# Pooled attention and a gated MLP on one core: the prologue as written words in another order, a packing product with its operands exchanged, a third output buffer, and shifted places in the later batches

## The chip, the cores and the metric

The kernel runs on one core of a Trainium2 chip. The metric is the device time of one execution in microseconds (us): for the kernel before, 744.43 as the median of three runs (742.96 to 745.0). The profile was taken from an execution of its own. TensorE (PE) multiplies matrices and writes to PSUM; VectorE (DVE) and ScalarE (ACT) read PSUM and SBUF; SyncE (SP) issues nearly all transfers.

## The reference

Eight batches of eight heads, 576 rows, head size 64, and 32 packing queries p per head, all float32:

```python
p_packed = sm_attn(p, k, v)          # softmax(p k^T / 8) v : 32 x 64 per head
out = sm_attn(q, p_packed, p_packed) # softmax(q p_packed^T / 8) p_packed : 576 x 64 per head
x = out.transpose(0, 2, 1, 3).reshape(4608, 512)
g = x @ w_gate                       # 512 x 1536
y = (g * sigmoid(g) * (x @ w_val)) @ w_out
```

## The kernel before

**Products without x.** The second softmax's weights a2 multiply p_packed, and that goes straight into w_gate and w_val. So the kernel forms m = p_packed times the weights for each batch (`m_mm`, L561) and then gate and value as m with a2 (`gv_chunk`, L602; `gv`, L788, for batch 0). The weights' 1536 columns are 12 chunks (`fc`); for each chunk a batch's 576 rows are done in two parts, A (256 columns of a2) and B (320). Then `silu`, the product with the value, and the product with w_out into four accumulators (`out_mm`, L633; `outs`, L836). Float32 accuracy comes from splitting each operand into a high and a low half (mh/ml, a2h/a2l, hh/hl, wo_h/wo_l) and adding three products; chunks 0 to 3 of batch 0 use the plain float32 product for gate and value (L801) and chunks 0 to 9 for w_out (L842). A plain product is issued as two instructions.

**Packing.** Batches 0 and 1 go by `s1_*`: scores with the 32 queries of each head on the partitions, their maximum, exp, transpositions on TensorE (`s1_turn`, L305, copied out by `s1_turned`), the product with v (`s1_pack`, L324), the sums, the division (`s1_scale`, L348), a transposition (`s1_flip`) and a copy (`s1_ppt`) into `ppt`. Batches 2 to 7 go by `q_*`: scores in four stretches of rows, maxima and sums kept by stretch (`q_sums`), gathered through DRAM (`q_gather`, L415), joined (`q_common`, L424), multiplied into the weights and transposed on VectorE in blocks of 32 (`q_turn`, L450), and then `q_pack` (L462): for each head pair (4) and each block of 32 rows (5), four products with the weights' block as stationary operand (128 rows by 32 columns) and 32 columns of v as moving operand. Each of the four writes its own 32 partitions of PSUM. VectorE transposes the result in blocks of 32 into `ppt`.

**Second softmax.** `s2_mm` (L487, two halves of 288 rows), `s2_block` (transposition of the scores by blocks), `s2_max`, `s2_exp`, `s2_sums`, `s2_scale`, and the transposition back. In batch 0 the latter is `back` (L768), which writes `a2f`.

**Weights.** They arrive as 64-bit floats. `f64_convert` (L181) makes float32 of a chunk in five steps, two on ScalarE (L187, L188) and three on VectorE (L189, L190, L191). In the written orders `W2` is the next step of chunk 2 of gate and value, `V0` of pair 0 of w_out.

**What sets the order.** Up to the end of batch 0 the orders of TensorE, VectorE, ScalarE and SP are those of the text. First come calls written one by one (L718 to L778), the prologue: loads, 8 warm-up matmuls of the identity with itself (`warm_up`, L702, each two instructions), the packing of batch 0, five steps of W0, the second softmax's first half, 18 more warm-ups. Then the words of `PROGRAM` (L40) are run in order (L896); its numbers say chunk, half or part. `g5` is the sixth gate-and-value part, `silu5` and `h5` its evaluation, `out5` its product with w_out, `M:1.0` a product m, `Mh:`/`Ml:` its high and low halves, `two_*` the second softmax of batch 0, `s1_*` and `s2_*` batch 1's, `warm25` 25 warm-ups.

From batch 1 on TensorE's order stays that of the text, and the other engines' instructions are ordered by a planner, save those held behind their predecessor in the text (`pin`, L154). The tables `FIRST` (for batch 2) and `LATER` (batches 3 to 7) say at which place of the batch before each part of a batch's attention is put: chunk and place within it, 1 and 2 in A's gate and value, a and ha behind A's silu and high half, 3 and 4 in A's out, 5 to 8, b and hb the same for B (`words2`, L650; `plan_of`, L685; called from `batch`, L912).

**Buffers.** PSUM has four accumulators, two `gv` and two `aux` buffers; while `wide` is true (the prologue) small products take accumulators and gv buffers in turn (`ps`, L158). Copies of finished accumulators go to `ot` (`emit_out`, L643), two buffers, and from there to DRAM.

Of the kernel before, what the change touches and what calls it, by code (L numbers as in the profile page):

```python
# [10 lines left out]
F32 = mybir.dt.float32  # L11
# [4 lines left out]
ALU = mybir.AluOpType  # L16
# [5 lines left out]
NP = 32  # L22
DM, DF = 512, 1536
P = 128
# [16 lines left out]
    W2 g0 W1 two_max1 two_high0 W2 warm25 W1 two_exp1 W2 W2 silu0 V0 h0 W2 V0 W1 load_w3 load_v1 M:1.0 two_sums1  # L41
    Mh:1.0 M:0.1 V0 Mh:0.1 two_scale1 g1 V0 silu1 two_back1 s1_scores0 h1 g2 two_high1 s1_max0 W3 V0 load_w4
    load_w5 silu2 W3 W3 out0 h2 s1_keep0 W3 g3 two_low1 silu3 W3 s1_scores1 load_wout1 load_w6 h3 g4 s1_max1 W4
    two_low0 out1 s1_top s1_keep1 W4 silu4 W4 h4 M:1.1 W5 W4 g5 Mh:1.1 W5 W5 W4 load_w7 out2 silu5 V1 h5 W5 out3
    V1 V1 g6 W5 load_wout2 W6 V1 silu6 M:2.2 W6 h6 g7 V1 load_w8 Mh:2.2 silu7 W6 W7 Ml:2.2 out5 W7 W7 h7 g8 V2 W7
    silu8 out4 V2 V2 W7 out6 W8 V2 W8 out7 W8 V2 g9 h8 s1_exp W6 out8 W6 load_w9 load_wout3 load_w10 W8 M:3.2
    silu9 h9 out9 Mh:3.2 W8 load_wout4 Ml:3.2 g10 silu10 s1_turn0 h10 g11 s1_turned0 W9 silu11 s1_turn1 W9 W9
    out10 h11 s1_turned1 W9 V3 out11 V3 V3 W9 load_w11 g12 W10 V3 M:4.2 silu12 W10 h12 g13 V3 load_q1 Mh:4.2 W10
    silu13 out12 V4 h13 Ml:4.2 V4 g14 V4 silu14 V4 W11 s1_turn2 out13 s1_turned2 h14 W11 W11 W10 s1_pack W10
    load_wout5 g15 s1_sums silu15 V4 load_k2 load_v2 out14 h15 W11 g16 silu16 W11 s1_flip out15 s1_ppt h16 V5  # L50
# [9 lines left out]
    0.b q0r  # L60
    0.hb q0s
    1.2 q0e
    1.ha q1 q1r
    2.a q1e
    2.7 q0z
    2.8 q1z
    3.2 common
    3.a common_e factors
    4.5 load_k
    4.b turn0  # L70
    4.hb turn1
    5.ha pack
    6.b load_v
    6.7 tiles
    7.ha mm0 block0
    7.3 max0
    8.a exp0 sums0
    8.7 turn_0
    9.ha mm1 block1
    9.3 high0 low0  # L80
    9.hb max1 exp1
    9.7 load_q
    9.8 sums1
    10.hb turn_1
    11.3 high1
    11.hb low1
# [18 lines left out]
    7.3 max0  # L105
    7.7 load_v
# [3 lines left out]
    9.a high0  # L110
    9.ha mm1 block1
    9.b low0
    9.hb max1 exp1
    9.7 load_q
    10.1 sums1
    10.hb turn_1
    10.8 high1
    11.4 low1
# [4 lines left out]
def tile_pack_attention_swiglu(ctx: ExitStack, tc: tile.TileContext, qT, kT, v, vq, pT, wgv, wout, out):  # L123
# [30 lines left out]
    def pin(ins):  # L154

        return tc.keep_in_program_order(ins) if steady[0] else ins
# [305 lines left out]
    def q_pack(b, bank=ps):  # L462

        p_p = bank()
        a1, v_t = sq[b][4], vs[b]
        for hp in range(NHP):
            for k in range(NKQ):
                for g in range(P // NP):
                    par, ds = g // 2, slice(g % 2 * NP, g % 2 * NP + NP)
                    nc.tensor.matmul(  # L470
                        p_p[NP * g : NP * g + NP, NP * hp : NP * hp + NP],
                        a1[:, par, hp, k, :], v_t[:, par, hp, k, ds],
                        start=(k == 0), stop=(k == NKQ - 1),
                    )
# [224 lines left out]
    with tc.manual_schedule(engines={mybir.EngineType.PE}):  # L699
# [15 lines left out]
        with tc.manual_schedule(  # L715
            engines={mybir.EngineType.DVE, mybir.EngineType.Activation, mybir.EngineType.SP}
        ):
            load_k(0)  # L718
            load_w(0)
            load_v(0)  # L720
            load_q(0)
            load_w(1)
            warm_up(8)
            s1_tile(0)
            for hf in range(2):
                s1_scores(0, hf)
                s1_max(0, hf)
            load_w(2)
            warm_up(6)
            s1_top(0)  # L730
            s1_exp(0, True)
            for x in range(NPAR + 1):
                s1_turn(0, x)
                s1_turned(0, x, nc.vector)
            s1_pack(0)
            s1_sums(0, True)
# [8 lines left out]
            for _ in range(4):  # L745
                step("W", 0)
            s1_scale(0)
            step("W", 0)
            s1_flip(0)
            s1_ppt(0)  # L750
            s2_tiles(0)
            c0, c1 = (slice(c, c + 1) for c in range(2))
            s2_mm(0, 0)
            s2_block(0, 0)
            m_mm(0, 0, c0, True)
            m_high(0, 0, c0)
            s2_max(0, c0)
            s2_exp(0, c0)
            s2_mm(0, 1)
            s2_block(0, 1)  # L760
            load_k(1)
            load_wout(0)
            warm_up(18)
            step("W", 1)
            step("W", 1)
            a2f = pool.tile([P, NPAR, S], F32, tag="a1", bufs=1, name="a2f")

            def back(c):  # L768
                for par in range(NPAR):
                    nc.vector.transpose(a2f[:, par, c * HS : (c + 1) * HS], st2[0][0][:, c, par])  # L770

            s2_sums(0, c0)
            s2_scale(0, c0)
            back(0)
            wide[0] = False

            t4_of(0)
            rows, accs = accs_of(0)  # L778
# [9 lines left out]
            def gv(i):  # L788
# [3 lines left out]
                if k < PLAIN:  # L792
                    terms = ((ms[0, k][0], a2f),)
# [53 lines left out]
            def a2_high(c):  # L847
                if c == 0:
                    s2_a2(0)
                nc.scalar.copy(a2[0][0][s2_at(c)], a2f[s2_at(c)])  # L850

            def a2_low(c):
                nc.vector.tensor_tensor(
                    a2[0][1][s2_at(c)], a2f[s2_at(c)], a2[0][0][s2_at(c)].bitcast(F32), op=ALU.subtract
                )
# [14 lines left out]
            def half_of(f, b):  # L870
# [7 lines left out]
                "g": gv, "silu": silu, "h": hmul, "hh": h_high, "hl": h_low, "out": outs,  # L878
                "W": lambda k: step("W", k), "V": lambda k: step("V", k),
# [149 lines left out]
```

## Time and profile before

| | |
|---|---|
| median of three runs | 744.43 us (742.96 to 745.0) |
| profiled execution, its time and its span | 742.52 us, 740.7 us |
| TensorE busy | 726.7 us, 98% |
| TensorE weight loads | 595.3 us, 80% |
| VectorE, ScalarE busy | 448.8 us (61%), 372.1 us (50%) |
| DMA traffic | 59.16 MB |
| granted TensorE clock | 1.000 |

A row of a group reads: line, engine, operation, output<-inputs, shapes, count. In a timeline the first two numbers are start and length in us; a bracket at the end holds the engine's idle time just before and what ended it. "issue" is idle time in which the engine waited for nothing that the profile shows. PEld is TensorE's loading of stationary operands, which runs beside the matmuls. In the chain of waits each row is start, length, and what was waited for.

### The profile page before, as it was taken

The page shows a single profiled execution, that of the slowest core. Times are in us where ns is not written, and L with a number is a line of the kernel's source. Part 1 is how long each engine was busy: PE and PEld are TensorE (multiplying, and loading weights), DVE is VectorE, ACT ScalarE, POOL GpSimd, SP SyncE. Part 2 cuts the span into 40 slices and gives each one's busy share as a digit, 9 for nine tenths or more (in the row PEclk, how much of TensorE's full clock was granted, in tenths as well). Part 3 has the DMA queues.
Part 4 walks back from the last instruction along what each step waited for, and adds up shares of the span by engine and source line. Part 5 has one row for each costly group of instructions (what it writes and reads, how often), then busy time and mean ns, then how long its engine had stood idle before and what let it go on. Part 6 is the DMA issues. An engine that isn't in the chain of part 4 may idle for free.

```text
span 740.7 us, 15176 instructions
## 1 busy us (share of the span) xinstructions
PE 726.7 (98%) x6288; PEld 595.3 (80%) x6288; DVE 448.8 (61%) x1008; ACT 372.1 (50%) x666; POOL 2.0 (0%) x13
## 2 busy tenths in 40 slices
PE   7999999999999999999999999999999999999997
PEld 5756667888888888888888888888888888888885
DVE  5988878675755557654665646655574545644333
ACT  3777745744635345553563536663553625533331
POOL 0000000000000000000000000000000000000000
PEclk9999999999999999999999999999999999999999
DMA  9686582310112201302112021102001000010001
GB/s 352 254 322 252 181 325 86 102 59 17 65 58 85 74 1 65 125 4 73 65 44 97 3 73 65 58 3 73 1 1 72 3 2 1 1 58 1 1 1 72
DMA packets 20005, 59.16 MB, mean 80 GB/s; under 512 B 5984, under 2 KB 7008, under 8 KB 17376
## 3 DMA queue, kind: packets, MB, share of 16 engines
q1 hardware_dynamic: 19792, 58.12, 21.7%
q8 instruction: 50, 0.82, 0.5%
q14 instruction: 19, 0.16, 0.1%
q10 hardware_dynamic: 144, 0.07, 0.0%
HBM read 48.69 MB, written 9.49 MB: 79 GB/s over the span
## 4 chain that ended last, share of the span: by engine, by line
PE 95%; DVE 2%; issue 1%; DMA 0%; ACT 0%; DVEq 0%; ACTq 0%
PE gv L616 36%; PE acc L635 33%; PE aux L257 7%; PE gv L801 6%; PE acc L842 4%; PE aux L635 4%; PE gv_aux L470 1%; PE gv_aux L257 1%; PE gv_aux L386 1%; PE acc L704 1%; DMA out<-ot 0%; DVE ot L170 0%; ACT mh L583 0%; PE aux L333 0%; DVE s L529 0%
## 5 line engine op out<-in xcount | busy, mean ns | idle before, releaser
L623 ACT ACTIVATE sg<-gv 128x256 f32<-128x256 f32 (+1 forms) x168 | 68.9, 410 | 173.8 <-PE gv L616 155.8
L627 DVE TENSOR_TENSOR hf<-gv,sg 128x256 f32<-128x256 f32 x168 | 71.0, 422 | 135.0 <-PE gv L616 116.6
L616 PE MATMUL gv<-a2h,ml 128*128 128x256 f32 (+1 forms) x672 | 143.9, 296 | 1.2 <-DVE t L826 1.2
L616 PE MATMUL gv<-a2h,mh 128*128 128x256 f32 (+1 forms) x672 | 144.1, 296 | 0.0
L616 PE MATMUL gv<-a2l,mh 128*128 128x256 f32 (+1 forms) x672 | 144.0, 296 | 0.0
L635 PE MATMUL acc<-wo_h,hl 128*128 128x512 f32 x344 | 140.7, 409 | 0.0
L635 PE MATMUL acc<-wo_l,hh 128*128 128x512 f32 x344 | 135.7, 395 | 0.0
L635 PE MATMUL acc<-wo_h,hh 128*128 128x512 f32 x344 | 134.7, 391 | 0.0
L616 PEld LDWEIGHTS gv<-a2h,ml 128*128 128x128 f32 x672 | 116.8, 189 | 16.3 <-issue 1.4
L168 ACT CAST hh<-hf 128x256 fp32r<-128x256 f32 x168 | 67.8, 404 | 106.4 <-DVE hf L627 106.3
L616 PEld LDWEIGHTS gv<-a2h,mh 128*128 128x128 f32 x672 | 108.6, 190 | 0.1
L616 PEld LDWEIGHTS gv<-a2l,mh 128*128 128x128 f32 x672 | 108.2, 189 | 0.0
L597 DVE TENSOR_TENSOR hl<-hf,hh 128x256 fp32r<-128x256 f32 x168 | 69.5, 414 | 37.6 <-ACT hh L168 37.6
L635 PEld LDWEIGHTS acc<-wo_h,hl 128*128 128x128 f32 x344 | 64.7, 188 | 27.6 <-issue 18.6
L635 PEld LDWEIGHTS acc<-wo_h,hh 128*128 128x128 f32 x344 | 64.6, 188 | 14.9
L635 PEld LDWEIGHTS acc<-wo_l,hh 128*128 128x128 f32 x344 | 64.8, 188 | 8.1 <-issue 0.5
L557 DVE TENSOR_TENSOR ml<-aux,mh 128x512 fp32r<-128x512 f32 x92 | 58.8, 680 | 2.4 <-ACT mh L583 2.4
L583 ACT CAST mh<-aux 128x512 fp32r<-128x512 f32 x92 | 49.4, 589 | 9.6 <-PE aux L257 4.3
L257 PE MATMUL aux<-w,ppt 64*32 64x512 f32 (+1 forms) x784 | 52.4, 588 | 0.5 <-ACT mh L583 0.5
L623 ACT ACT_TABLE_LOAD x30 | 38.5, 1283 | 12.3 <-PE gv L616 11.8
L842 PE MATMUL acc<-wo_f,h 128*128 128x512 f32 x80 | 37.2, 595 | 0.0
L842 PEld LDWEIGHTS acc<-wo_f,h 128*128 128x128 f32 x80 | 14.3, 189 | 13.8 <-issue 13.2
(152 smaller groups left out, 754.7 us busy)
## 6 DMA issues: line engine op xcount, KB each, us to landing
st<-in_wgv SPq DMA_DIRECT2D x12, 1024.0 KB, 6.5
k_t<-in_kT SPq DMA_DIRECT2D x16, 576.0 KB, 5.1
q_t<-in_qT SPq DMA_DIRECT2D x16, 576.0 KB, 4.8
out<-ot SPq DMA_DIRECT2D x36, 256.0 KB, 2.1
v_t<-in_vq SPq DMA_DIRECT2D x6, 1280.0 KB, 5.9
st<-in_wout SPq DMA_DIRECT2D x6, 1024.0 KB, 5.5
v_t<-in_v SPq DMA_DIRECT2D x2, 1024.0 KB, 8.7
p_t<-in_pT SPq DMA_DIRECT2D x7, 64.0 KB, 2.6
```

Of the source, the lines that this page charges most:

```text
L168: e.copy(dst, src)
L257: nc.tensor.matmul(outs[par][32 * hp : 32 * hp + 32], lhs(r, hp), rhs(r, hp), start=True, stop=True)
L386: nc.tensor.matmul(pss[par][NP * j : NP * j + NP, i * SQ : (i + 1) * SQ], p_t[r, 2 * g + i, :], k_t[r, j // 2, 2 * g + i, j % 2 * SQ : j % ...
L557: pin(nc.vector.tensor_tensor(*lows.pop(0), op=ALU.subtract))
L583: nc.scalar.copy(m[0][at], src)
L597: low = lo.tensor_tensor(hl, src, hh.bitcast(F32), op=ALU.subtract)
L616: nc.tensor.matmul(pg[:, :n], m_[:, g, f, s * P : (s + 1) * P], a_[:, g, off : off + n], start=(i == 0), stop=(i == 5),)
L623: nc.scalar.activation(sg[:, :n], pgs[0][:, :n], AF.Silu)
L627: nc.vector.tensor_tensor(hf, pgs[1][:, o : o + 256], sg[:, o : o + 256], op=ALU.mult)
L635: nc.tensor.matmul(acc[:, :], h_[:, c : c + P], w_[fc // 2][:, fc % 2], start=(fc == 0 and i == 0), stop=(fc == NFC - 1 and i == 2),)
L801: nc.tensor.matmul(held[i][s][:, :n], m_[:, g, f, s * P : (s + 1) * P], a_[:, g, off : off + n], start=(j == 0), stop=(j == len(todo) - 1),)
L842: nc.tensor.matmul(accs[2 * is_b + c], half(i)[:, c * P : c * P + P], wos[fc // 2][:, fc % 2], start=(fc == 0), stop=(fc == NFC - 1),)
```

## The change

1. The prologue's calls become words at the head of `PROGRAM` (`z_*` for batch 0's packing, `two_mm`, `two_block`, `heat` for the warm-ups, `narrow` for the end of the wide use of PSUM), and the whole order is another one. `back` makes its tile when first called.
2. `q_pack` takes v as stationary operand (128 rows by 64 columns) and the weights' block as moving operand (32 columns), so that the product comes out transposed; a copy replaces VectorE's transposition.
3. `ot` has three buffers.
4. `FIRST` and `LATER` hold other places.

```diff
 PROGRAM = """
-    W2 g0 W1 two_max1 two_high0 W2 warm25 W1 two_exp1 W2 W2 silu0 V0 h0 W2 V0 W1 load_w3 load_v1 M:1.0 two_sums1
-    Mh:1.0 M:0.1 V0 Mh:0.1 two_scale1 g1 V0 silu1 two_back1 s1_scores0 h1 g2 two_high1 s1_max0 W3 V0 load_w4
...
-    M:5.2 wout_high0 V5 g17 wout_high1 wout_low0 wout_high2 wout_low1 silu17 wout_low2 V5 out16 h17 Mh:5.2 V5 g18
-    wout_high3 Ml:5.2 silu18 out17 h18 V5 g19 wout_low3 silu19 wout_high10 s2_mm0 h19 g20 s2_block0 silu20
-    wout_high11 s2_mm1 load_q2 h20 hh20 wout_low10 s2_max0 g21 hl20 silu21 out19 h21 hh21 s2_block1 out20 s2_max1
-    s2_exp0 wout_low11 s2_exp1 hl21 s2_sums1 g22 M:6.2 s2_back1 silu22 out18 Mh:6.2 h22 hh22 s2_sums0 s2_high1
-    out21 Ml:6.2 hl22 s2_low1 g23 s2_back0 silu23 h23 hh23 s2_high0 hl23 s2_low0
+    load_k0 load_w0 load_v0 load_q0 z_scores0 z_scores1 z_max0 z_max1 z_top heat8 load_w1 load_w2 load_k1 heat6
+    z_exp z_turn0 z_turned0 z_turn1 z_turned1 z_turn2 W0 W0 z_turned2 z_sums W0 load_wout0 z_pack z_scale z_flip
+    W0 z_ppt two_mm1 two_mm0 W0 two_block0 two_max0 two_exp0 two_block1 two_sums0 M:0.0 two_scale0 heat18 narrow
+    two_max1 W1 Mh:0.0 W1 W2 two_back0 g0 W1 two_exp1 two_high0 W2 W2 silu0 V0 W1 V0 W2 load_v1 W2 warm25 W1
+    load_w3 M:1.0 M:0.1 two_sums1 h0 two_scale1 Mh:1.0 V0 Mh:0.1 two_back1 g1 s1_scores0 silu1 load_w5 V0 g2
...
+    M:5.2 out16 Mh:5.2 g18 silu18 h17 Ml:5.2 wout_low2 h18 g19 wout_low3 V5 s2_mm0 silu19 g20 wout_high10 h19
+    wout_low1 wout_high11 load_q2 silu20 s2_block0 g21 h20 wout_low10 hh20 s2_mm1 silu21 hl20 s2_max0 h21 hh21
+    s2_block1 out19 g22 s2_max1 s2_exp1 s2_exp0 wout_low11 out20 s2_sums1 hl21 silu22 out17 s2_back1 M:6.2 out18
+    Mh:6.2 s2_high1 h22 g23 s2_sums0 s2_low1 silu23 Ml:6.2 h23 hh22 s2_back0 hh23 hl23 s2_high0 hl22 s2_low0
+    out21
 """
 FIRST = """
...
+    1.6 q0z
     2.a q1e
-    2.7 q0z
-    2.8 q1z
-    3.2 common
+    2.4 q1z
+    3.a common
...
 LATER = """
...
-    1.4 q0z
     2.a q1e
-    2.4 q1z
-    3.ha common
-    3.5 common_e
-    3.hb factors
-    4.a turn0
-    4.4 load_k
-    4.5 turn1
+    2.6 q0z
+    2.b q1z
+    2.7 common
+    3.2 common_e
+    3.4 factors
+    3.7 load_k turn0
+    4.ha turn1
     5.ha pack
...
@@ def q_pack
-                for g in range(P // NP):
-                    par, ds = g // 2, slice(g % 2 * NP, g % 2 * NP + NP)
+                for par in range(NPAR):
                     nc.tensor.matmul(
-                        p_p[NP * g : NP * g + NP, NP * hp : NP * hp + NP],
-                        a1[:, par, hp, k, :], v_t[:, par, hp, k, ds],
+                        p_p[D * par : D * par + D, NP * hp : NP * hp + NP],
+                        v_t[:, par, hp, k, :], a1[:, par, hp, k, :],
                         start=(k == 0), stop=(k == NKQ - 1),
                     )
         ppts[b] = pool.tile([P, P], F32, tag="ppt", bufs=2, name="ppt")
-        pin(nc.vector.transpose(ppts[b], p_p[:, :P]))
+        pin(nc.vector.tensor_copy(ppts[b], p_p[:, :P]))
@@ def emit_out
-        ot = pool.tile([P, DM], F32, tag="ot", bufs=2, name="ot")
+        ot = pool.tile([P, DM], F32, tag="ot", bufs=3, name="ot")
@@ the prologue's calls go; in their place
+            def narrow(_):
+                wide[0] = False
+                t4_of(0)
+                for x, y in zip((rows, accs), accs_of(0)):
+                    x.extend(y)
...
+                "z_scores": lambda x: (None if x else s1_tile(0), s1_scores(0, x)), "z_max": lambda x: s1_max(0, x),
...
+                "two_block": lambda c: s2_block(0, c), "narrow": narrow, "heat": warm_up,
```

In `FIRST` the places of turn0 to low1 move by at most one chunk as well (load_k from 4.5 to 5.b, load_v from 6.b to 6.a), in `LATER` those from max0 to low1 (load_v from 7.7 to 8.2, high1 from 10.8 to 11.1, low1 from 11.4 to 11.8). The places of TensorE's words (q0, q1, pack, mm0, mm1) are the same.

More of the change, by code (lines that the diff above doesn't have):

```diff
@@ L46 @@
[L46 to L50, printed above, removed]
@@ L59 @@
     0.2 q0
[L60 to L63, printed above, removed]
+    0.4 q0r
+    0.b q0s
+    1.ha q1 q0e q1r
+    1.6 q0z
     2.a q1e
-    2.7 q0z
-    2.8 q1z
-    3.2 common
-    3.a common_e factors
-    4.5 load_k
-    4.b turn0
+    2.4 q1z
+    3.a common
+    3.4 common_e
+    4.2 factors
+    4.5 turn0
     4.hb turn1
     5.ha pack
-    6.b load_v
-    6.7 tiles
+    5.b load_k
+    6.a load_v
+    6.8 tiles
     7.ha mm0 block0
-    7.3 max0
-    8.a exp0 sums0
-    8.7 turn_0
+    7.hb max0
+    7.8 exp0
+    8.1 sums0
+    8.8 load_q
     9.ha mm1 block1
[L80 to L86, printed above, removed]
+    9.3 turn_0
+    9.5 high0
+    9.hb max1
+    10.1 exp1
+    10.2 sums1
+    10.ha low0
+    10.8 turn_1
+    11.4 high1
+    11.5 low1
 """
@@ L104 @@
     7.ha mm0 block0
-    7.3 max0
-    7.7 load_v
+    7.5 max0
+    8.2 load_v
     8.a exp0
@@ L109 @@
     8.hb turn_0
-    9.a high0
     9.ha mm1 block1
+    9.5 high0
+    9.6 load_q
     9.b low0
[L113 to L118, printed above, removed]
+    9.7 max1
+    10.1 exp1
+    10.ha sums1
+    11.1 turn_1 high1
+    11.8 low1
 """
@@ L717, in tile_pack_attention_swiglu @@
         ):
[L718 to L736, printed above, removed]
             conv = {}
@@ L743, in step @@
                 next(conv[kind, k], None)
[L745 to L766, printed above, removed]
+            a2fs = []
             def back(c):
+                if not a2fs:
+                    a2fs.append(pool.tile([P, NPAR, S], F32, tag="a1", bufs=1, name="a2f"))
                 for par in range(NPAR):
[L770 to L778, printed above, removed]
+                    nc.vector.transpose(a2fs[0][:, par, c * HS : (c + 1) * HS], st2[0][0][:, c, par])
+            rows, accs = [], []
+            def narrow(_):
[3 more added lines that the diff above has]
+                    x.extend(y)
             SPLIT = NFC // 2 - 1
@@ L792, in gv @@
                 if k < PLAIN:
-                    terms = ((ms[0, k][0], a2f),)
+                    terms = ((ms[0, k][0], a2fs[0]),)
                 else:
```

20 lines of the change are left out of this document (15 added, 5 removed).

## The prediction

> **What bounds the kernel now.** I read the page first, then the busy time by stage, then who waits for whom on TensorE, then the chain of waits through the first 34 us, then single stretches.
>
> ```profile
> span 740.7 us, 15176 instructions
> ...
> PE 726.7 (98%) x6288; PEld 595.3 (80%) x6288; DVE 448.8 (61%) x1008; ACT 372.1 (50%) x666; POOL 2.0 (0%) x13
> ```
> ```profile
> 34.00:122.80 88.80, 88.80 (x591) 1.00 0.68 252
> ...
> 124.30:729.80 605.50, 603.07 (x5341) 1.00 0.13 43
> ```
> Columns of the second fence: stretch, its length, TensorE's busy time and instructions, granted clock, DMA share, GB/s. From 34.00 on TensorE is never free but for four holes; the view of its waits from 115 us on names them (total, times, longest):
>
> ```profile
> PE gv_aux L470 <- issue: 2.4, 2, 1.3
> PE gv L616 <- DVE t L826: 1.2, 1, 1.2
> PE aux L635 <- DVE hl L597: 1.0, 1, 1.0
> ```
> So an edit counts in three ways only: it moves the moment at which TensorE's unbroken stream begins, it changes the length of TensorE's own instructions, or it opens or shuts such a hole.
>
> **The packing product (L470).** Six batches, 160 instructions each now (80 products, each issued as two), 32 stationary columns and 32 moving; 80 each later, with 64 stationary columns. Undisturbed, and twice with a stop:
>
> ```profile
> 251.85 1.56 PE L470 MATMUL gv_aux<-v_t,a 128*32 128x32 f32 x160
> 253.34 0.50 PE L635 MATMUL acc<-wo_h,hl 128*128 128x512 f32 x1
> ```
> ```profile
> 159.75 1.35 PE L470 MATMUL gv_aux<-v_t,a 128*32 128x32 f32 x135
> 162.21 0.40 PE L470 MATMUL gv_aux<-v_t,a 128*32 128x32 f32 x25 [1.11 <-issue]
> 162.54 0.50 PE L635 MATMUL acc<-wo_h,hl 128*128 128x512 f32 x1
> ```
> ```profile
> 598.84 1.40 PE L470 MATMUL gv_aux<-v_t,a 128*32 128x32 f32 x141
> 601.53 0.38 PE L470 MATMUL gv_aux<-v_t,a 128*32 128x32 f32 x19 [1.29 <-issue]
> 601.84 0.50 PE L635 MATMUL acc<-wo_h,hl 128*128 128x512 f32 x1
> ```
> Start to next start: 253.34 - 251.85 = 1.49, 162.54 - 159.75 = 2.79, 601.84 - 598.84 = 3.00. Four groups of columns work side by side, so each takes 40 instructions in 1.49: at most 37 ns apiece. Does halving the instructions halve this? With 64 columns two groups remain, and each still takes 40. What matters is what one instruction costs its group:
>
> ```profile
> L470 PEld LDWEIGHTS gv_aux<-v_t,a x960: 106/109/113, 159.7 to 601.7; 128*32 128x32 f32 x192
> ```
> ```profile
> L704 PEld LDWEIGHTS acc<-ident x50: 190/192/192, 23.8 to 29.4; 128*128 128x128 f32 x50
> ```
> ```profile
> 88.58 1.73 PE L333 MATMUL aux<-v_t,a 128*32 128x64 f32 x80
> 90.24 0.56 PE L801 MATMUL gv<-a2h,mh 128*128 128x320 f32 x2
> ```
> A weight load's median grows from 109 ns at 32 columns to 192 at 128, (192 - 109)/96 = 0.86 ns a column. Streaming is no dearer: L333 has 20 instructions a group, 64 moving, in 90.24 - 88.58 = 1.66, so at most 83 ns for 64 moving, stops included. The 50 warm-up instructions of L704 (128 by 128; chain row below) take 5.58/50 = 112 ns, which is the load's 0.86 x 128 = 110 and a little. 32 columns by that law are 28 ns and a little, against 34 to 37 seen. I take it that the load sets the pace; 64 columns are 0.86 x 64 + 4 = 59 ns, 40 x 59 = 2.36, with the 0.1 until the next line 2.45 a batch. **Price:** 6 x 2.45 = 14.7 against 4 x 1.49 + 2.79 + 3.00 = 11.75, +2.9. The stops (2.79 + 3.00 - 2 x 1.49 = 2.8) are in that: they come some 135 instructions into the burst with no semaphore ahead, so instructions ran short, and at a third of the rate I expect none. Bounds: 1.4 a batch if streaming alone set the pace, -3.3; 2.45 with the stops kept, +5.7. The copy that replaces the transposition afterwards is of the same 128x128 on VectorE, off the path.
>
> [...]
>
> **The front.** Chain of waits now (start, length, what):
>
> ```profile
> 13.31 1.23 DVE w L190
> 14.54 0.21 DVE pp L350
> ...
> 15.48 0.43 PE gv_aux L257
> ...
> 16.31 0.84 DVE s L497 x2
> ...
> 17.17 0.76 DVE r L511
> ...
> 17.95 0.77 DVE s L512
> ...
> 19.52 0.76 DVE r L523
> ...
> 20.82 0.77 DVE s L529
> ...
> 22.24 1.97 PE gv L801 x8
> 24.20 5.58 PE acc L704 x50
> 29.79 0.70 PE aux L257 x16
> ...
> 32.33 1.99 PE gv L801 x8
> ```
> From g0 (22.24) TensorE goes through g0, the 50 warm-ups and the M words to g1; both orders have these in line, and from then on it is full, so each us by which g0 moves is a us of the end. From the end of the scale (14.75) g0 starts 7.5 later now. In the new order VectorE does behind the scale: both last steps of W0 (2 x 1.2, one of them ahead of the scale now), block0 0.84, max0 0.78 + 0.77, block1 0.84 (covering exp0), sums0 1.30 (19.52 to 20.82), scale0 0.79, then **max1**, which stood behind g0, and a first transposition of back0, 0.6:
>
> ```profile
> 22.95 0.74 DVE L511 TENSOR_REDUCE r<-s 128x18 f32<-128x576 f32 x1
> 23.72 0.76 DVE L512 TENSOR_TENSOR s<-s,r 128x576 f32<-128x576 f32 x1
> ```
> Max1 is 1.45. Sum: 2.4 + 0.84 + 1.55 + 0.84 + 1.3 + 0.79 + 1.45 + 0.6 = 9.8, so +2.3. On TensorE M:0.0 now waits for a buffer that block1 reads (about 5.2 behind the scale), then the 36 warm-ups (36 x 0.112 = 4.0) end at 9.9, no later than back0. W1 and W2 need six VectorE steps behind g0 (2 x 0.6 + 4 x 1.15 = 5.8), under g0 and the warm-ups' 7.5: free.
>
> Ahead of the scale the warm-ups move:
>
> ```profile
> 1.35 3.78 PE L704 MATMUL warm_ps<-ident 128*128 128x128 f32 x16 [1.35 <-POOL ident masks.py:199]
> ```
> ```profile
> 7.09 1.60 PE L704 MATMUL warm_ps<-ident 128*128 128x128 f32 x12
> ```
> The first 16 took 236 ns each, the later 12 took 133, most of them 112: TensorE starts at half pace. The 16 ran while k was still loading and cost nothing. Now all 28 stand between the scores (over at about 7.4, 0.3 later than today's 7.09 for running slowly) and the first z_turn, and nothing has sped TensorE up before. All quick, 28 x 0.112 = 3.1, they end at 10.5; all slow, 28 x 0.22 = 6.2, at 13.6; in the old order some 5 us of work went by before the quick pace (1.35 to between 5.1 and 7.3), so I take 11.5, slow for about a third of them. Behind it come z_turn, three copies, the pack and the scale:
>
> ```profile
> 11.14 0.69 DVE L170 COPY a<-gv_aux 128x512 f32<-128x512 f32 x1 [0.27 <-PE gv_aux L314]
> ```
> ```profile
> 11.93 1.88 PE L333 MATMUL gv_aux<-v_t,a 128*32 128x64 f32 x80 [0.60 <-DVE a L170]
> ```
> The turn's four at 0.11 and its pipeline are 0.6, the copies 0.6, 0.6 and 0.4 (0.69 each less what they overlap, the third of half the size), the part of the pack's 1.88 that needs the third copy 1.3, the scale 0.25: 3.8. So the scale ends at 15.3 instead of 14.75, +0.5; at best at 14.1, since the pack's end at 13.81 (11.93 + 1.88) waits for v and a, at worst at 17.4 (-0.6 to +2.6). **Front: +2.8** (+1.7 to +4.9).
>
> **Rest of batch 0.** The hole of 1.2 at 123.03 is VectorE late with g23's product. The new order puts out20, out17, M:6.2 and out18 between g22 and g23, where M:6.2, out18 and out21 stood, and out21 behind g23; a plain out (out17, out18) is
>
> ```profile
> 56.97 1.72 PE acc L842 x4
> ```
> and a split one (out20, out21) 6 x 0.23 = 1.4, so 5.8 of TensorE stand there instead of 4.1, and 1.4 more behind g23. VectorE's list up to h23 (sums0, low1, the low halves of M:6.2) thus gets 3.1 more before batch 1 asks for g23's buffer, which it missed by 1.2: -1.2. In return g18/g19 and g20/g21 stand back to back, with a silu needed between: +0.4 (0 to 1.5).
>
> **Third output buffer.** At the end VectorE waits for the first store before its second copy, and a high half for TensorE stands behind that copy:
>
> ```profile
> 729.76 0.69 DVE L170 COPY ot<-acc 128x512 f32<-128x512 f32 x1 [3.66 <-DMA out<-ot]
> ```
> A third buffer lets this copy run at once; the hole of 1.0 goes: -1.0.
>
> **The other tables.** TensorE's words keep their places in both, so TensorE's order past batch 0 is the same; VectorE and ScalarE words and loads move by about a place, inside slack (VectorE is 61% busy, ScalarE 50%, by the page). 0, at worst +8 (second rival).
>
> **Sum:** +2.9 + 2.8 - 0.8 - 1.0 = +3.9. The profiled execution took 742.5 (span 740.7 and 1.8 around it); its median neighbours 744.43, 1.9 above. 742.5 + 3.9 = 746.4 for its like, **748.3** as a median.
>
> **Rivals.** (1) *A 64-column load is as quick as a 32-column one*, since four groups load side by side already. Then the product is -3.3 instead of +2.9: 744.43 - 2.3 = 742.1, and faster by over 0.3% where the front comes out at its low end (741.0). For: the groups' independence. Against: the slope of load lengths. (2) *The gather wait.* In the later table q1z stands at 2.b and its reader common at 2.7, one place on; today 2.4 and 3.ha:
>
> ```profile
> 323.18 0.21 DVE L430 TENSOR_REDUCE y<-x 128x8 f32<-128x32 f32 x1 [2.47 <-DMA x<-zd]
> ```
> VectorE then would stand up to 4 us in five batches, with hf behind it, which TensorE's two gv buffers need within about 3.5; 1.5 a batch lost is 748.3 + 7.5 = 756. Against: batch 2's old table has 2.8 and 3.2, as close, and only 5 of the 6 commons waited, so independent work is let past. (3) *TensorE slows down again.* Between two_mm0 and M:0.0 it now has about 3.1 idle; at the start pace the 36 warm-ups cost 36 x 0.1 = 3.7 more: 752. The longest hole behind the start is today's 1.29 at 600, so no row decides. [...] (4) *The front is no later*, because the warm-ups end quickly and VectorE finds room I missed: 748.3 - 2.8 = 745.5.
>
> **How the numbers follow.** Forecast 0.52, rivals 0.18, 0.10, 0.12, 0.08. 0.3% is 2.2 us, about what a measurement of this kernel can tell from no change: 742.2 to 746.7 counts as none. The forecast's own range is 745.5 to 751.5 (front and product bounds): 0.40 slower, 0.12 no change. Rivals 2 and 3 add 0.22 to slower. Rival 1 is 0.13 faster and 0.05 no change; of rival 4, 0.03 comes together with rival 1 (739.3) and 0.05 without. Faster 0.16, same 0.22, slower 0.62. The range 741.5 to 753 reaches to rivals 1, 3 and 4 and leaves out rival 2 and the far ends.
>
> **What would show it.** Product: start to next start about 2.45, 80 instructions, loads near 136 ns, no issue stop; at 1.4 rival 1 holds. Front: g0 near 25, g1 near 35. Tail and 123: no hole over 0.3. VectorE's wait for x far above 2.5 with holes at L616 is rival 2. The forecast is wrong if g0 comes by 23, or the product costs under 1.9.

## The result, and the profile after

The changed kernel takes 748.41 us (median of four runs, 747.78 to 748.61). The kernel before, run beside it, takes 743.98 (742.96 to 745.0). The ratio is 1.0053, with a 95% interval of 1.0035 to 1.0071: **slower by 4.4 us**. The profiled execution took 748.36 (span 746.6), 5.84 more than the one of before.

First the profile's page for the changed kernel:

```profile
span 746.6 us, 14224 instructions
...
PE 732.8 (98%) x5808; PEld 601.6 (81%) x5808; DVE 454.2 (61%) x1008; ACT 372.5 (50%) x666; POOL 2.0 (0%) x13
```

TensorE has 480 matmuls fewer and is busy 6.1 us longer. Busy time by stage (stretch, its length, TensorE's busy time and instructions, the same for the other engines, granted clock, DMA share, GB/s):

```profile
34.30:123.60 89.30, 88.29 (x594) 55.47 (x595) 74.33 (x121) 62.77 (x94) 0.00 (x0) 1.00 0.66 238
126.00:740.00 614.00, 614.00 (x4883) 521.96 (x4882) 352.23 (x836) 291.85 (x543) 1.23 (x6) 1.00 0.13 43
```

The two holes of 0.5 ahead of the second gate-and-value part (L770; `g1`) lie in the first stretch. The waits of 1.2 at 123 and of 1.0 at the end and the issue stops in the packing product are gone; from 126 on there is not one hole left. The end came later all the same, so the time went into the front and into TensorE's own instructions.

**The packing product** (timeline of TensorE, then its weight loads as shortest/median/longest in ns):

```profile
162.46 2.52 PE L476 MATMUL gv_aux<-a,v_t 128*64 128x32 f32 x80
164.91 0.50 PE L641 MATMUL acc<-wo_h,hl 128*128 128x512 f32 x1
```
```profile
L476 PEld LDWEIGHTS gv_aux<-a,v_t x480: 132/138/138, 162.5 to 608.1; 128*64 128x64 f32 x160
```

Start to next start is 2.45, as in all six batches (2.45 or 2.46).

**The front** in the changed kernel, timeline of TensorE, then of VectorE:

```profile
17.75 0.40 PE L264 MATMUL gv_aux<-w,ppt 64*32 64x256 f32 x1 [0.90 <-DVE s L503]
...
18.34 4.29 PE L710 MATMUL warm_ps<-ident 128*128 128x128 f32 x36
24.50 2.84 PE L770 MATMUL gv<-a2f,mh 128*128 128x256 f32 x8 [1.87 <-DVE a2f L738]
27.13 6.57 PE L710 MATMUL acc<-ident 128*128 128x128 f32 x50
...
36.24 1.13 PE L770 MATMUL gv<-a2f,mh 128*128 128x256 f32 x4 [0.50 <-ACT mh L589]
```
```profile
14.62 0.29 DVE L357 TENSOR_TENSOR pp<-gv_aux,rs 128x128 f32<-128x128 f32 x1 [0.21 <-PE gv_aux L340]
...
17.22 0.48 DVE L503 STREAM_TRANSPOSE s<-gv_aux 128x288 f32<-128x288 f32 x1
...
22.42 0.74 DVE L517 TENSOR_REDUCE r<-s 128x18 f32<-128x576 f32 x1
23.20 0.76 DVE L518 TENSOR_TENSOR s<-s,r 128x576 f32<-128x576 f32 x1
23.88 0.83 DVE L738 STREAM_TRANSPOSE a2f<-s 128x288 f32<-128x288 f32 x2
```

The scale (`pp`) ends at 14.91 (14.74 before), g0 starts at 24.50 (22.24), g1 at 36.24 (32.33). Max1 (L517, L518) stands ahead of the transposition for which g0 waits. But g0 took 2.84 instead of 1.97, and the 50 warm-ups 6.57 instead of the 5.74 that the same view has for the kernel before (24.04 on). The busy time by stage of the changed kernel there tells why:

```profile
22.00:25.43 3.43, 1.56 (x10) 1.30 (x9) 3.40 (x7) 3.38 (x5) 0.00 (x0) 1.00 1.04 414
25.43:28.84 3.41, 3.41 (x14) 3.05 (x12) 3.38 (x4) 3.38 (x4) 0.00 (x0) 0.50 0.65 256
```

The last column but two is the granted clock. It is 0.50 for one stretch of 3.41 us, right behind a stretch in which TensorE was busy 1.56 of 3.43, and 1.00 again from 28.84 on.

In sums, over the two profiled executions, from the starts of the instructions at the borders of the stages (us):

| stage | before | after | difference |
|---|---|---|---|
| to the end of the scale | 14.74 | 14.91 | +0.17 |
| scale to g1 | 17.59 | 21.33 | +3.74 |
| g1 to the first packing product | 127.42 | 126.22 | -1.20 |
| six packing products | 11.75 | 14.74 | +2.99 |
| between the products, five stretches | 430.34 | 431.10 | +0.76 |
| last product to the last matmul's end | 135.18 | 134.50 | -0.68 |
| **sum** | **737.02** | **742.80** | **+5.78** |

### The profile page after: what moved, and what is told of

It is laid out like the page before. It is cut to its first block, busy times and chain, and to the rows that moved or that the text cites. A ratio compares the mean times of both kernels' runs of the same rounds, so it can differ in the third digit from the quotient of the medians.

```text
span 746.6 us, 14224 instructions
## 1 busy us (share of the span) xinstructions
PE 732.8 (98%) x5808; PEld 601.6 (81%) x5808; DVE 454.2 (61%) x1008; ACT 372.5 (50%) x666; POOL 2.0 (0%) x13
## 4 chain that ended last, share of the span: by engine, by line
PE 97%; DVE 1%; DMA 1%; ACT 0%; issue 0%; DVEq 0%; ACTq 0%
PE gv L622 36%; PE acc L641 33%; PE aux L264 7%; PE gv L770 6%; PE acc L811 5%; PE aux L641 4%; PE gv_aux L476 2%; PE acc L710 1%; PE gv_aux L393 1%; PE gv_aux L264 1%; DMA p_t<-in_pT 1%; PE warm_ps L710 1%; PE acc_aux L264 0%; PE aux L340 0%; DVE a L177 0%; DVE s L518 0%
```

## The experiments

Each was timed beside the kernel before, whose medians were 743.27 (beside e1 to e4), 743.32 (e5 to e8) and 743.24 (e9 to e12). The first table is by times, the second by stages of the profiled execution, worked out as above. "Rest" is the length of the first stretch between two products. "Full clock from" is the moment at which the profile first records the full clock.

| kernel | median | ratio, interval | above before |
|---|---|---|---|
| changed kernel | 748.41 | 1.0053, 1.0035 to 1.0071 | +4.4 |
| e1 swap alone | 744.36 | 1.0011, 1.0001 to 1.0021 | +1.1 |
| e2 old product | 745.92 | 1.0036, 1.0023 to 1.0049 | +2.7 |
| e3 hole filled | 747.69 | 1.0058, 1.0043 to 1.0073 | +4.4 |
| e4 max1 behind | 746.08 | 1.0038, 1.0023 to 1.0053 | +2.8 |
| e5 third buffer alone | 741.76 | 0.9978, 0.9966 to 0.9990 | -1.6 |
| e6 old tables | 748.15 | 1.0060, 1.0043 to 1.0078 | +4.8 |
| e7 double moving | 748.52 | 1.0066, 1.0046 to 1.0086 | +5.2 |
| e8 order alone | 746.77 | 1.0044, 1.0028 to 1.0061 | +3.5 |
| e9 warm-ups first | 746.23 | 1.0038, 1.0023 to 1.0052 | +3.0 |
| e10 end of batch 0 | 742.17 | 0.9987, 0.9975 to 0.9999 | -1.1 |
| e11 three undone | 743.08 | 0.9999, 0.9990 to 1.0007 | -0.2 |
| e12 end and filler | 744.88 | 1.0019, 1.0007 to 1.0032 | +1.6 |

| kernel | full clock from | scale ends | scale to g1 | half clock later | six products | rest |
|---|---|---|---|---|---|---|
| before | 6.3 | 14.74 | 17.59 | no | 11.75 | 89.31 |
| changed | 8.4 | 14.91 | 21.33 | 25.4 to 28.8 | 14.74 | 89.58 |
| e1 | 6.8 | 14.73 | 18.47 | 17.1 to 20.5 | 14.71 | 89.30 |
| e2 | 11.0 | 16.22 | 19.67 | no | 11.94 | 89.62 |
| e3 | 10.5 | 15.97 | 19.67 | no | 14.72 | 89.60 |
| e4 | 8.7 | 15.01 | 18.59 | no | 14.74 | 89.60 |
| e5 | 5.6 | 14.78 | 18.07 | 15.8 to 19.2 | 11.74 | 89.27 |
| e6 | 10.7 | 16.04 | 19.68 | no | 14.75 | 89.67 |
| e7 | 11.6 | 16.47 | 19.68 | no | 14.88 | 89.60 |
| e8 | 11.2 | 16.19 | 19.67 | no | 11.91 | 89.64 |
| e9 | 6.1 | 13.94 | 19.80 | no | 14.72 | 89.59 |
| e10 | 5.0 | 15.48 | 19.27 | 11.8 to 22.0 | 11.50 | 89.31 |
| e11 | 5.3 | 13.85 | 18.66 | no | 12.76 | 89.58 |
| e12 | 6.2 | 14.59 | 17.59 | no | 12.50 | 89.30 |

### The packing product: e1, e2, e7

e1 is the kernel before with the new `q_pack` alone; e2 is the changed kernel with the old one.

> The kernel before with the exchanged packing product alone. If the weight load paces the product (64 columns, about 59 ns for each of 40 in a group), each of the six products takes 2.45 to 2.46 us from its start to the next line instead of 1.49, both stops vanish, and the time is 2.9 to 3.0 us above the kernel before (14.73 against 11.75). If the product were slow only because of what else the change does (order, tables), it stays near 1.4 to 1.5 here and the time falls by about 3 us.

> The changed kernel with the old packing product put back. Load theory: each product 1.49 us again, 5.8 us off in all, less the stops that come back: none to four of them at 1.3 to 1.5 each, so 0 to 5.8 us below the changed kernel, 3 to 5 the likeliest. [...]

The six products take 14.71 in e1 and 11.94 in e2: the swap costs 2.8 to 3.0 wherever it stands. The stops come and go with it (TensorE's waits from 115 us on; total, times, longest), all that e2 has, then all that e1 has:

```profile
PE gv_aux L477 <- issue: 2.6, 2, 1.5
PE gv L623 <- issue: 0.3, 1, 0.3
```
```profile
PE gv L615 <- DVE t L825: 1.2, 1, 1.2
```

In time e1 loses only 1.1, because it wins elsewhere too: its end from the last product on is 133.93 long against 135.18, and the wait of 1.0 for `hl` that the prediction quoted is gone without any third buffer. Why the swap ends that wait is open.

e7 is the changed kernel with each moving block taken twice (64 columns of output, half of them not used):

```diff
-                        v_t[:, par, hp, k, :], a1[:, par, hp, k, :],
+                        v_t[:, par, hp, k, :], a1[:, par, hp, k, :].unsqueeze(1).broadcast_to([P, 2, NP]),
```

> The changed kernel with the moving block of the packing product taken twice over, 64 moving columns instead of 32 beside the same 64 stationary ones; each product is computed in two copies and the first is used. Load theory: streaming 64 columns takes 56 ns as in the product of batch 1, still under the load's 59, so each product stays at 2.45 to 2.55 us and the time at that of the changed kernel within 0.6. If streaming or the product as a whole set the pace, each product grows to 3.5 to 4.7 us and the time by 6 to 13.

TensorE's timeline in e7:

```profile
254.45 2.55 PE L476 MATMUL gv_aux<-a,v_t 128*64 128x64 f32 x80
256.93 0.50 PE L644 MATMUL acc<-wo_h,hl 128*128 128x512 f32 x1
```

2.48 against 2.46: twice the moving columns cost 0.02. So what sets the pace of 59 to 62 ns an instruction is the stationary side, whose 64 columns both kernels load.

### The front: e8, e3, e4, e9

e8 is the kernel before with the new prologue and order alone (old product, old tables, two buffers).

> The kernel before with the prologue and batch 0 in the new written order alone (old product, two output buffers, old tables). By the two traces: the front costs 3.9 (2.3 of it VectorE's longer list before g0, 1.65 the half clock), the hole at the end of batch 0 gives 1.2 back, so 2.7 above the kernel before, give or take the stops of the packing product, which move with the count of instructions (two of 1.3 to 1.5 before): 0 to 4. If the order's loss and the other parts' do not add up, it lies outside that.

It is 3.5 slower, so most of the loss is in the order. But its front is not that of the changed kernel: no half clock behind g0, and a later scale, as VectorE's timeline in e8 has it:

```profile
15.89 0.29 DVE L355 TENSOR_TENSOR pp<-gv_aux,rs 128x128 f32<-128x128 f32 x1 [0.21 <-PE gv_aux L338]
```

The same holds for e2, e3, e6 and e7. In all of these the full clock came at 10.5 to 11.6, in the changed kernel's profile at 8.4, and the later it came, the later, on the whole, the scale ended. Behind the scale all five need the same 19.67 or 19.68 up to g1. So the front has a fixed part, 19.67 - 17.59 = 2.08, and a part that depends on the clock: either a late full clock (1.2 to 1.7 ahead of the scale) or an early one and half a clock later (0.17 + 1.66). Which of the two a profile shows looks like chance and not like a matter of these edits, which leave all words up to the scale alone; what decides it was not shown. In the profiles it hardly matters: g1 comes at 35.64 to 36.15 in the five and at 36.24 in the changed kernel.

e3 fills the hole ahead of g0 with 8 more warm-ups (16 instructions).

```diff
-... M:0.0 two_scale0 heat18 narrow
+... M:0.0 two_scale0 heat26 narrow
```

> The changed kernel with 26 warm-ups instead of 18 in the word heat18, so that TensorE has work until just before g0. Clock theory: g0 starts at 24.5 as now, but g0 and the 50 warm-ups behind it run at the full clock, the first M:1.0 starts 1.6 to 1.7 us earlier (at about 32.0 instead of 33.6) and the time falls by 1.6 us. Rival: g0 was slow for its own sake (its operands, traffic); then nothing moves, or g0 starts later by what the warm-ups overrun.

TensorE's timeline in e3:

```profile
19.40 6.07 PE L710 MATMUL warm_ps<-ident 128*128 128x128 f32 x52
25.55 1.97 PE L770 MATMUL gv<-a2f,mh 128*128 128x256 f32 x8
```

The hole is gone, and g0 is no earlier: 9.58 behind the scale against 9.59. g0 waits for VectorE, not for TensorE. The time is that of the changed kernel (+4.4). What a filled hole can win is the half clock, and with a full clock as late as 10.5 that was not to be had: e2, e6, e7 and e8 kept the hole and had none. What a filled hole wins after an early full clock, as in the changed kernel's profile, was not measured.

e4 puts max1 behind g0.

```diff
-    two_max1 W1 Mh:0.0 W1 W2 two_back0 g0 W1 two_exp1 ...
+    W1 Mh:0.0 W1 W2 two_back0 g0 W1 two_max1 two_exp1 ...
```

> The changed kernel with two_max1 moved back behind g0 and W1's third step, where it stood before. Theory of the prediction: g0 starts 1.45 us earlier (at about 23.05), and everything behind by as much. Because TensorE's hole before g0 shrinks from 1.9 to 0.4, the half clock goes too if it came from the hole: 1.45 + 1.65 = 3.1 us off. If the half clock has another cause, 1.45 off. If VectorE's later steps (W1, W2) pace the M words, less than 1.45.

TensorE's timeline in e4:

```profile
23.26 1.97 PE L770 MATMUL gv<-a2f,mh 128*128 128x256 f32 x8 [0.54 <-ACT st L195]
```

Scale to g1 falls from 19.67 to 18.59, so max1 is 1.1 of the fixed 2.1. The hole shrinks from 1.87 to 0.54, and with the full clock from 8.7 on no half clock follows. The time is 1.6 nearer to the kernel before than the changed kernel's (2.5 between the two profiled executions, 1.66 of it the half clock).

e9 puts the first 8 warm-ups ahead of the scores again.

```diff
-    load_k0 load_w0 load_v0 load_q0 z_scores0 z_scores1 z_max0 z_max1 z_top heat8 load_w1 ...
+    load_k0 load_w0 load_v0 load_q0 heat8 z_scores0 z_scores1 z_max0 z_max1 z_top load_w1 ...
```

> The changed kernel with one word moved: the first 8 warm-ups (16 instructions) stand ahead of the scores again, as in the kernel before. In the runs with the new order the full clock came 8.4 to 11.6 us after the start and the scale ended at 14.9 to 16.5; in those with the old one it came at 5.6 to 6.8 and the scale ended at 14.73 to 14.78. Theory (the late warm-ups let the clock come late): full clock by 7, scale end 14.6 to 14.9, the second gate-and-value part at scale end + 19.7 = 34.3 to 34.6, up to 0.9 later where a window of half clock falls between 15 and 21; time 0.5 to 1.5 us less than the changed kernel's, ratio to the kernel before 1.0035 to 1.005. Rival (the delay ahead of the scale is in the order of the other engines): scale end stays at 15.5 or more, ratio 1.005 to 1.006.

Timelines: TensorE's first instruction in the changed kernel, then TensorE's in e9, then the scale on VectorE in e9:

```profile
5.05 0.68 PE L264 MATMUL acc_aux<-k_t,p_t 64*32 64x288 f32 x1 [5.05 <-DMA p_t<-in_pT]
```
```profile
1.35 3.78 PE L710 MATMUL warm_ps<-ident 128*128 128x128 f32 x16 [1.35 <-POOL ident masks.py:199]
```
```profile
13.65 0.29 DVE L357 TENSOR_TENSOR pp<-gv_aux,rs 128x128 f32<-128x128 f32 x1 [0.57 <-PE gv_aux L340]
```

The full clock comes at 6.1, and the scale ends at 13.94, 0.7 earlier than expected and 0.8 earlier than in the kernel before. There a step of W0 stood right ahead of the scale (13.31 and 14.54 in the prediction's chain of waits); the new order has that step behind it, and the scale waits only for its product. So of the 2.08 that the new order needs more behind the scale, 0.8 would come back ahead of it if the clock came in time. g1 is at 33.74, and the time is 1.4 nearer to the kernel before (2.5 between the profiled executions, 1.66 of it again the half clock). So the late warm-ups were a cost of the new order, and the rival, other engines' order ahead of the scale, falls.

### The end of batch 0: e10

e10 is the kernel before with the third buffer and one part of the new order.

```diff
-... h21 hh21 s2_block1 out20 s2_max1 ... g22 M:6.2 ... s2_high1 out21 Ml:6.2 ... hl23 s2_low0
+... h21 hh21 s2_block1 s2_max1 ... g22 out20 M:6.2 ... s2_high1 Ml:6.2 ... hl23 s2_low0 out21
```

> The kernel before with the third output buffer, and of the new order only the end of batch 0: out20 stands behind g22, out21 behind all the rest. Theory (TensorE work between g22 and batch 1 covers VectorE's list): the hole of 1.2 at 123 is gone, the rest as with the third buffer alone, so 1.2 us less than that kernel: ratio 0.9962 (0.995 to 0.9975). Rival (the hole goes elsewhere, because g23's product waits for the same VectorE list): ratio 0.998, a hole over 0.5 between 115 and 126. The 0.2 to 0.3 us by which every later batch was longer in all kernels with the new order: if the end of batch 0 brings it, batch lengths here without the packing product are 89.6 and 81.2, if not 89.3 and 81.0.

TensorE's waits in e10 from 60 us on have:

```profile
PE gv L616 <- DVE t L826: 1.2, 1, 1.2
```

The hole stands, at 125.4 and 1.21 long: the rival was right, though the ratio is 0.9987 and not its 0.998. Moving TensorE's words behind g22 adds no TensorE work ahead of batch 1, it only moves it; what counts is when VectorE's list ends. (The batches' rest is 89.31 here: this part of the order does not lengthen them.)

What can have shortened that list in the new order stands in the words. In the old one `s2_back0`, a scaling and a transposition on VectorE, stands ahead of `h23`, whose last instruction (`t`) frees the buffer that batch 1 asks for; in the new one `h23` stands first. VectorE's timeline in the kernel before, then in the changed kernel:

```profile
122.08 0.75 DVE L529 TENSOR_TENSOR s<-s,r 128x576 f32<-128x576 f32 x1
122.86 0.78 DVE L538 STREAM_TRANSPOSE t<-s 128x576 f32<-128x576 f32 x1
...
123.88 0.21 DVE L826 TENSOR_TENSOR t<-gv,sg 128x64 f32<-128x64 f32 x1
```
```profile
125.37 0.22 DVE L795 TENSOR_TENSOR t<-gv,sg 128x64 f32<-128x64 f32 x1
125.50 0.75 DVE L535 TENSOR_TENSOR s<-s,r 128x576 f32<-128x576 f32 x1
126.28 0.78 DVE L544 STREAM_TRANSPOSE t<-s 128x576 f32<-128x576 f32 x1
```

That takes 123.57 - 122.08 = 1.49 out of VectorE's list ahead of the buffer, more than the hole of 1.2. VectorE also waits less between 98 and 127 us, 3.3 in all instead of 5.4. Every kernel with the new order is without the hole, and every one with the old end (e1, e5, e10, e12) has it. Neither difference was tried by itself.

### The third buffer and the tables: e5, e6

e5 is the kernel before with `bufs=3` for `ot`, e6 the changed kernel with the old `FIRST` and `LATER`.

> The kernel before with the third output buffer alone. Theory: the copy at the end no longer waits for the first store, TensorE's hole of about 1.0 us near the end goes, the time falls by 1.0 us, and nothing else moves. Rival: the hole only moves to another wait (the store after it, or the second half's copy) and the gain is under 0.4.

> The changed kernel with the two old tables of places. Theory: TensorE's order is the same, so within 0.3 us of the changed kernel. If the small growth seen between the packing products of the later batches (some 0.1 to 0.3 us a batch, 0.8 in all) comes from the new tables, 0.5 to 0.9 below it. If the new tables hide a loss of another part, above it.

In e5 TensorE's waits from 115 us on are these; the wait for `hl` at the end is gone:

```profile
PE gv_aux L470 <- issue: 2.4, 2, 1.3
PE gv L616 <- DVE t L826: 1.2, 1, 1.2
PE gv L616 <- issue: 0.3, 1, 0.3
```

From the last product on it takes 133.95 instead of 135.18, and the kernel 1.6 less than before: **this one beats both kernels**, if only by 0.22% (0.10 to 0.34). e6 is no different from the changed kernel in time, and behind g1 no stage differs by more than 0.3: the tables are worth nothing that can be seen.

### Do the parts add up: e11, e12

e11 undoes three parts of the changed kernel: warm-ups first, max1 behind, old product.

> The changed kernel with three of its parts undone: first warm-ups ahead of the scores, max1 behind g0, old packing product. If the parts add up: 1.0 (warm-ups) + 2.1 (max1) + 2.5 (product) = 5.6 us less than the changed kernel, that is 0.6 to 1.5 under the kernel before: ratio 0.998 to 0.9995. If they overlap (the front is bound by VectorE whatever the clock): ratio 1.000 to 1.0025.

It comes out at the time of the kernel before, between the two expectations. The front gives 36.24 - 32.51 = 3.7 in the profiles, the product only 14.74 - 12.76 = 2.0 instead of the 3.0 between the changed kernel and the one before, since the stops grew:

```profile
PE gv_aux L477 <- issue: 3.4, 2, 1.8
```

e12 is e10 with 8 more warm-up instructions ahead of the scaled pack.

```diff
             s1_scale(0)
+            warm_up(4)
             step("W", 0)
```

> As the kernel with the end of batch 0 rearranged and the third buffer, and 4 more warm-ups (8 instructions, 0.9 us) in the 1.05 us in which TensorE waits for the scaled pack at 13.8. Theory (the clock halves after a window of 3.41 us in which TensorE was busy less than 60%): no window of half clock before the end, mean granted clock 1.0 in nearly all executions, 0.3 to 0.8 us less than without the filler in the median. Rival (the window is set by something else): half clock from about 16 to 20 again in some executions, same time within 0.2.

Neither expectation held in time. (The 60% of the theory is read from profiles: the clock stayed full after 60% in the kernel before and halved after 59% in e5; last section.) The profiled execution had no half clock and the shortest front of all (g1 at 32.18), though some of the other executions did have half clock (mean granted clock 0.995 to 1.0); yet the kernel is 2.7 slower than e10. TensorE's waits from 60 us on, e12 first, then e10:

```profile
PE gv_aux L470 <- issue: 2.9, 2, 1.5
PE acc L635 <- issue: 1.6, 1, 1.6
...
PE gv L802 <- DVE t L827: 0.7, 1, 0.7
```
```profile
PE gv_aux L470 <- issue: 2.1, 2, 1.1
...
```

Behind g1 the profile of e12 is 3.3 longer than that of e10. With 8 more warm-up instructions in the front the issue stops far behind it are 2.4 longer (4.5 against 2.1), and 0.7 is a wait for VectorE that e10 does not have. Why the added instructions lengthen the stops is not shown.

## Why the prediction was right, and where not

The forecast was 748.3, slower, and 748.41 was measured. The verdict and the sizes of two terms (the packing product and the tables) were right; that the number fits to a tenth is luck, since two errors cancelled.

**The error that cancelled.** Like for like the sum said +3.9 over the profiled execution, 746.4; measured was 748.36, +5.84. The step "its median neighbours 744.43, 1.9 above" then added 1.9 for the changed kernel too. Its executions do not lie above its profiled one (748.36 against a median of 748.41). The profiled execution of before had no half clock at all; e1 and e5, with the same front, had one near 16 to 20 and needed 18.07 and 18.47 from scale to g1 instead of 17.59. So it was one of its quicker executions for a reason that the changed kernel does not share. Most of the 1.9 was also a small sample: beside the experiments 55 executions of the kernel before have a median of 743.24, those with a mean granted clock of 0.999 or more (24) 742.9, those with 0.997 or less (23) 743.7. The difference of the medians is +4.4 against the four executions beside the changed kernel and +5.2 against the 55, which is within the interval.

**Packing product, predicted +2.9, measured +2.99.** Every part held: 2.45 a batch, a load near 136 ns (138), no stop at a third of the rate. The reason held too: e7 took streaming out of the question. Rival 1 (1.4 a batch) fell. That the groups work side by side shows in the starts of the loads: in the kernel before (251.84 on) they come in fours, 6 to 7 ns from one to the next and 28 to 32 from four to four at first; in the changed kernel (162.46 on) in pairs, 6 to 7 ns and 55 to 59. Over the whole product an instruction of a group takes 2.46/40 = 61 with the ends, against the 59 of the prediction.

**Front, predicted +2.8, measured +3.91.** The term was mis-sized in three places.
- Behind the scale VectorE's list was to cost +2.3; it is 2.08, the same in five kernels, 1.1 of it max1 (e4), which the prediction had at its whole length of 1.45.
- Ahead of the scale +0.5 was taken, -0.6 to +2.6 as bounds. It was +0.17 here, and 1.2 to 1.7 where the full clock came later; e9 shows that the moved warm-ups are the cause, as the prediction had it.
- The step that failed is that "M:0.0 now waits for a buffer that block1 reads", with the warm-ups ending "no later than back0". M:0.0 started at 17.75, 2.84 behind the scale, not 5.2: the first transposition of block0 (17.22, L503) had freed its buffer. So the 36 warm-ups ended 1.87 ahead of g0, not with it. The hole by itself costs nothing (e3), but in this execution it fell into a stretch in which TensorE was busy 45%, and the half clock that followed cost 21.33 - 19.67 = 1.66, 0.87 of it in g0 and the rest in the warm-ups. The sum had nothing for this.

**Rival 3 came true in another place.** It put the slowing into an idle of 3.1 between two_mm0 and M:0.0, which came out as 0.90, and asked 3.7 for it. It happened ahead of g0, behind a stretch of 3.43 that was 45% busy, and cost 1.66. Rival 4 (a front no later) fell: g0 came 2.26 later.

**Rest of batch 0, predicted -0.8, measured -1.20.** The hole went as forecast, but the step by which VectorE's list "thus gets 3.1 more before batch 1 asks for g23's buffer" is wrong: e10 moved out20 and out21 (1.4 of the 3.1) and kept the hole at its full length. The prediction's list up to h23 left out `s2_back0`, which the new order puts behind h23; these 1.49 of VectorE's time are what the traces show in its place, though no run moved them alone. That the hole went was right by luck. The +0.4 for the parts that stand back to back did not show: -1.20 is the hole alone.

**Third buffer, predicted -1.0.** The hole of 0.95 at the end went, and e5 alone is 1.6 quicker. In the changed kernel the buffer is probably not worth that: the swap alone (e1) ends the same wait, and the order alone (e8) shrinks it to 0.2, but no run takes the buffer out of the changed kernel. The end is 0.68 shorter and not 1.2 as in e5, for the reason given below.

**Tables, predicted 0.** Right (e6). Rival 2 fell: VectorE waits 0.5 for x in the whole changed kernel, against 7.9 before.

**Not in the sum: TensorE's own products past batch 0, some 1.8.** The prediction took TensorE's work past batch 0 as unchanged, since its words keep their places. The table has +0.76 between the products, but there the kernel before has a third stretch that is 0.36 longer than its like (89.67 against 89.31; last section). Against e1, which has no issue stop, the changed kernel is 431.10 - 429.87 = 1.23 longer between the products and 134.50 - 133.93 = 0.57 longer behind them. The rest of a batch is 89.6 instead of 89.3 in every kernel with the new order (e2, e3, e4, e6 to e9, e11) and in no other. The w_out products take it. TensorE's busy time in that line alone, over one batch and its next product (stretch, length, TensorE and loads), e1 and then the changed kernel:

```profile
335.81:427.56 91.75, 46.18 (x180) 32.41 (x180) 1.00 0.16 57
```
```profile
338.15:430.16 92.01, 46.50 (x180) 32.47 (x180) 1.00 0.16 57
```

It is 0.32 more for the same 180 instructions, at full clock and without a hole. It is not the tables (e6), not the product (e2, e8) and not the place of out20 and out21 (e10). Which part of the order does it, and how, stays open.

## What to carry to other kernels

Before you swap the operands of a small product, price the load of what becomes stationary: halving the instructions and doubling the stationary columns won nothing here (a load's median went from 109 to 138 ns, the six products from 11.75 to 14.74), though it ended all stops. Where TensorE waits on another engine, look at the share in which it is busy, stretch by stretch, and not only at the longest hole: here half clock came behind a stretch of 3.43 that was 45% busy and cost 1.66. Start the warm-ups as early as what they read allows: e9 came 1.4 nearer to the kernel before by it. Compare a profiled execution with a median only after asking which clock it had.

## What the runs showed of the hardware

**Half clock came behind stretches of 3.4 us in which TensorE was busy 45 to 59%.** In the changed kernel the granted clock is 0.50 from 25.43 to 28.84, 3.41 us, and in e1 from 17.05 to 20.46, 3.41 again. The first full clock came anywhere from 5.0 to 6.8 with one and the same front (before, e1, e5, e10), and the next change 17.05 - 6.81 = 10.24 later in e1, which is 3 x 3.41, and 25.43 - 8.37 = 17.06 later in the changed kernel, 5 x 3.41. In the changed kernel the clock halves after 1.56 of 3.43 (45%). The kernel before stays at full clock after 60%, e9 after 61%:

```profile
13.20:16.60 3.40, 2.05 (x68) 0.88 (x57) 2.89 (x5) 0.27 (x1) 0.00 (x0) 1.00 1.05 428
```
```profile
19.70:23.10 3.40, 2.08 (x19) 1.89 (x17) 3.26 (x7) 3.40 (x5) 0.00 (x0) 1.00 1.02 411
```

e5 halves after 59%, e1 after 52%:

```profile
12.40:15.80 3.40, 2.00 (x83) 1.27 (x76) 3.26 (x6) 0.67 (x2) 0.00 (x0) 1.00 1.04 426
15.80:19.20 3.40, 3.40 (x52) 1.65 (x37) 2.68 (x6) 0.76 (x3) 0.00 (x0) 0.50 1.00 408
```
```profile
13.60:17.05 3.45, 1.78 (x43) 0.72 (x49) 3.04 (x5) 0.56 (x3) 0.00 (x0) 1.00 1.03 422
17.05:20.46 3.41, 3.41 (x28) 2.65 (x13) 3.25 (x7) 2.01 (x5) 0.00 (x0) 0.50 0.98 362
```

In e10 the clock halves after 58%. It stays at half after stretches that are 83% and 80% busy at half clock, and is back after one that is 100% busy:

```profile
8.40:11.80 3.40, 1.97 (x10) 1.00 (x10) 1.70 (x4) 3.40 (x10) 0.00 (x0) 1.00 1.00 369
11.80:15.20 3.40, 2.83 (x80) 2.11 (x80) 2.23 (x7) 0.58 (x1) 0.00 (x0) 0.50 1.05 404
15.20:18.60 3.40, 2.71 (x41) 1.08 (x49) 2.31 (x5) 0.34 (x2) 0.00 (x0) 0.50 1.01 412
18.60:22.00 3.40, 3.40 (x28) 2.65 (x13) 3.25 (x7) 2.38 (x5) 0.00 (x0) 0.50 0.64 190
22.00:25.40 3.40, 3.40 (x30) 3.32 (x29) 3.30 (x7) 3.40 (x4) 0.00 (x0) 0.99 1.02 353
```

So the fullest of these stretches that lost the full clock was 59% busy and the emptiest that kept it 60%; at half clock 83% did not bring it back and 100% did. In the kernel before and in the changed kernel no other stretch of 3.41 at full clock, counted from the changes of clock up to 35 us, was less than 60% busy, and none lost it. At the start the first full clock followed 3.33 of 3.41 (98%, 2.93 to 6.34) in the kernel before and 3.28 of 3.42 (96%, 4.95 to 8.37) in the changed kernel. The busy time is modelled, so these shares are rough, and what makes the clock change no run shows.

**The issue stops came at the same count of instructions in seven kernels.** Counted in the traces, TensorE's instructions (matmuls, weight loads and semaphore instructions) ahead of the two stops in the packing product are 2753 and 10945 in all of before, e2, e5, e8, e10, e11 and e12, though e12 has 16 more ahead of the product. A third, near 340 us, stands at 6081 in e2, e5 and e12; in the kernel before the matmul with this number comes 0.19 late, too little for the view of waits. What TensorE waits for at these counts no view names. The count does not set the length of a stop by itself: e11 has e2's counts, and its two stops in the product are 3.4 long against 2.6.
